# A constant's tile in front of the second layer's small tiles made 256 bytes wide instead of 128

## The chip, the core and the metric

The kernel runs on one core of a Trainium2 chip. The metric is the device time of one execution in microseconds (us), the median of several runs. TensorE (PE in the profile) multiplies matrices, VectorE (DVE), ScalarE (ACT) and GpSimd (POOL) work on elements, and SyncE (SP) issues nearly all DMAs. SBUF, the memory on the chip, has 128 partitions. A tile begins at the same byte in each of its partitions, and that byte is all that this change moves.

## The reference, cut to what matters

```python
B, H, S, Ns, D = (8, 8, 512, 32, 64)
...
x = np.ascontiguousarray(attn_out.transpose(0, 2, 1, 3)).reshape(B * S, H * D)   # 4352 x 512
...
a = x @ w1                       # first layer: 512 -> 1024
b = x @ w2
h = a * b @ w3
x = h @ w_out                    # -> 512
...
h = x @ w_in                     # second layer: 512 -> 2048
relu6 = np.clip(h + 3.0, 0.0, 6.0)
g = h * relu6 / 6.0
return (g @ w_out).astype(np.float32)
```

Attention of 8 batches gives 8 blocks of 512 token rows and 256 state rows. All products are in fp32 accuracy: an operand is split into a high and a low part (names that end in h and l), and three matmuls (high by high, high by low, low by high) take the place of one.

## The kernel before, in words

The program has two stages on TensorE. Up to about 555 us stand the attention, the conversion of the weights and the first layer; its tiles are named Ah, Al, ph, pl, ab, abh, abl, w3ph, w3pl. From about 556 us on stands the second layer, and the change is there.

The second layer takes the blocks of 512 rows in pairs (four values of p) and the 2048 columns of the hidden size in 8 pieces (g), so it runs through 32 units n = 8p + g, and one more (n = LAST = 32). A unit has two parts, which the source writes out in the order in which TensorE executes them:

- Seven products, `prod` (line 799, matmul at line 804), in a scheme with seven products for a block of two by two. Each is six matmuls of 128x128 weights by 512 columns: the weights are slices of `wh` and `wl`, the streamed operand is `xc`, the sum goes to a PSUM bank. In the trace these are `ps<-xc,wh` and `ps<-xc,wl`: the streamed operand stands first, the weights second.
- Eight output groups, `out_mm` (line 840), of the unit before: six matmuls each by `mm3` (lines 88 to 90). Here the weights are 128-column slices of `g`, the high or low part of the gated hidden values, and the streamed operand is `woh` or `wol`, the second weight matrix. In the trace: `ps_o<-woh,g` and `ps_o<-wol,g`. VectorE then adds the bank to the tile `oa` (`add`, line 808), or ScalarE copies it there the first time (line 854).

Six of the eight output groups follow a product directly (`T_()`), one at a time; the last two follow the sixth (`T_(8)`), so three stand in a row. Then come the first two products of the next unit. From n = 25 on the state rows are done too: `state_h` (half-width products, `ps_hs`) and two more groups a unit whose weights are `gs` instead of `g` (`ps_o<-woh,gs`, same lines, same streamed tiles).

The gate is `chain` (line 812): ScalarE's Relu with the bias `half` into `rl`, VectorE's minimum and product into `gt`, ScalarE's rounding to the high part `g`, VectorE's subtraction for the low part. The tiles m1, m5 (`m`), u2, u3 (`u`), `c`, `rl`, `gt`, `g` and `oa` are the small tiles: 512 fp32 values, 2048 bytes a partition each, all from the pool `pb`, which lays its tiles one behind the other in the order of first use. `half` stands in front of them and behind the weights. Its tile is 32 fp32 values wide, and one column of it is used.

Where tiles begin, in bytes in a partition, in the built program:

| tile | begins at (first buffer) | modulo 256 |
|---|---|---|
| first layer: w3ph, w3pl, ph, pl, Ah, Al, asb, ab, abh, abl, x2s | 49280, ... | 128, all |
| wh, wl | 16512, 30848 | 128 |
| woh, wol | 45184, 53376 | 128 |
| half | 61568 | 128 |
| m1, m5, u2, rl, gt, u3, c | 61696, 63744, 65792, 67840, 71936, 76032, 78080 | 0 |
| g (16 buffers) | 84224 to 114944 | 0 |
| oa (10 buffers) | 116992 to 135424 | 0 |
| xc, gs (from the pool xb, at the other end) | 163712, 196480 | 128 |

A 128-column slice of fp32 values is 512 bytes, so a slice of a tile begins in the same place modulo 256 as the tile.

Of the kernel before, what the change touches and what calls it, by code (L numbers as in the profile page):

```python
# [7 lines left out]
F32 = mybir.dt.float32  # L8
# [11 lines left out]
def attn_moe_kernel(tc, xt_d, xn_d, bd_d, wa, wb, wc, wi, wo, out):  # L20
# [32 lines left out]
    def open_pool(key, **kw):  # L53
        es[key] = ExitStack()
        return es[key].enter_context(tc.tile_pool(name=key, **kw))
# [284 lines left out]
    with tc.manual_schedule():  # L340
# [242 lines left out]
        def x2_load(p):  # L583
            if p < B // 2:
                x2r[p] = r = [xb.tile([128, 2, 512], F32, tag=f"r{i}", name=f"r{i}") for i in range(4)]
                for i in range(4):
                    nc.sync.dma_start(out=r[i], in_=x2d[2 * p + i % 2][:, i // 2 * 2:i // 2 * 2 + 2, :])
# [186 lines left out]
        pb = open_pool("pb", bufs=1, side=left, reuse_waits="tile")  # L774
# [17 lines left out]
        wo_load(0)  # L792
        w_load(1)
        x2_load(1)
        half = pb.tile([128, 32], F32, name="half")[:, :1]
        nc.vector.memset(half, 0.5)
        A11, A12, A22, S1, S2, S3, S4 = range(7)

# [245 lines left out]
```

## Time and profile before

| | |
|---|---|
| median of 3 runs | 1275.61 us (1274.97 to 1275.72) |
| profiled execution, first to last instruction | 1274.1 us |
| median of the runs less that span | 1.5 us |
| PE busy | 1237.6 us (97%) |
| DVE busy | 858.0 us (67%) |
| ACT busy | 518.7 us (41%) |
| POOL busy | 32.2 us (3%) |
| granted TensorE clock, mean | 0.993 of full speed |
| DMA moved | 202.67 MB, mean 159 GB/s |

Busy shares are of the whole span. Matmuls overlap: the next starts while the last one is still draining, so the time that one takes (some 390 ns for 512 columns) is longer than the distance from its start to the next start, and that distance is what a row of matmuls costs. The chain of waits shows a matmul with this distance. Times from the span's start are given to 0.01 us.

### The profile page before, as it was taken

The page shows a single profiled execution, that of the slowest core. Times are in us where ns is not written, and L with a number is a line of the kernel's source. Part 1 is how long each engine was busy: PE and PEld are TensorE (multiplying, and loading weights), DVE is VectorE, ACT ScalarE, POOL GpSimd, SP SyncE. Part 2 cuts the span into 40 slices and gives each one's busy share as a digit, 9 for nine tenths or more (in the row PEclk, how much of TensorE's full clock was granted, in tenths as well). Part 3 has the DMA queues.
Part 4 walks back from the last instruction along what each step waited for, and adds up shares of the span by engine and source line. Part 5 has one row for each costly group of instructions (what it writes and reads, how often), then busy time and mean ns, then how long its engine had stood idle before and what let it go on. Part 6 is the DMA issues. An engine that isn't in the chain of part 4 may idle for free.

```text
span 1274.1 us, 16840 instructions
## 1 busy us (share of the span) xinstructions
PE 1237.6 (97%) x6784; PEld 972.2 (76%) x6784; DVE 858.0 (67%) x1268; ACT 518.7 (41%) x811; POOL 32.2 (3%) x18
## 2 busy tenths in 40 slices
PE   5989999999999999999999999999999999999997
PEld 2446787777777788778888888888888888888885
DVE  7976877786877643645667847578566696555664
ACT  3434545464554542544234443234433344332330
POOL 0000000000000000000000200002000030000000
PEclk9989999999999999999999999999999999999999
DMA  9741554554554211354434554345624254342223
GB/s 362 274 166 67 214 211 162 201 227 170 213 189 150 88 37 59 131 175 168 178 114 159 208 198 149 124 160 194 226 99 182 91 190 165 131 141 92 91 91 116
DMA packets 49589, 202.67 MB, mean 159 GB/s; under 512 B 9192, under 2 KB 11240, under 8 KB 42856
## 3 DMA queue, kind: packets, MB, share of 16 engines
q1 hardware_dynamic: 48936, 200.56, 43.5%
q8 instruction: 53, 0.87, 0.3%
q10 hardware_dynamic: 576, 1.05, 0.2%
q14 instruction: 24, 0.20, 0.0%
HBM read 160.17 MB, written 41.42 MB: 158 GB/s over the span
## 4 chain that ended last, share of the span: by engine, by line
PE 85%; DVE 9%; ACT 2%; DMA 1%; issue 1%; ACTq 0%; DVEq 0%; SPq 0%
PE ps L804 24%; PE ps_o L88 10%; PE ps_o L90 10%; PE ps_o L89 10%; PE x L88 4%; PE x L89 4%; PE x L90 4%; PE ps_ab L88 4%; PE ps_ab L90 4%; PE ps_ab L89 4%; PE ps_p L360 2%; PE ps_hs L804 2%; PE ps_w L414 1%; PE ps_r L228 1%; DVE ab L508 1%
## 5 line engine op out<-in xcount | busy, mean ns | idle before, releaser
L804 PE MATMUL ps<-xc,wh 128*128 128x512 f32 x896 | 276.6, 390 | 0.0
L808 DVE TENSOR_TENSOR oa<-oa,ps_o 128x512 f32<-128x512 f32 x238 | 162.9, 686 | 165.8 <-PE ps_o L90 165.1
L88 PE MATMUL ps_o<-woh,g 128*128 128x512 f32 x512 | 203.3, 397 | 0.3 <-ACT g L71 0.3
L90 PE MATMUL ps_o<-woh,g 128*128 128x512 f32 x512 | 201.8, 394 | 0.0
L89 PE MATMUL ps_o<-wol,g 128*128 128x512 f32 x512 | 201.4, 393 | 0.0
L804 PEld LDWEIGHTS ps<-xc,wh 128*128 128x128 f32 x896 | 168.3, 188 | 36.3
L804 PE MATMUL ps<-xc,wl 128*128 128x512 f32 x448 | 175.6, 392 | 0.0
L71 ACT ACTIVATE g<-gt 128x512 fp32r<-128x512 f32 x128 | 81.1, 634 | 177.6 <-DVE gt L818 177.5
L90 PEld LDWEIGHTS ps_o<-woh,g 128*128 128x128 f32 x512 | 96.3, 188 | 23.8 <-DVE g L79 0.4
L89 PEld LDWEIGHTS ps_o<-wol,g 128*128 128x128 f32 x512 | 96.9, 189 | 21.5
L88 PEld LDWEIGHTS ps_o<-woh,g 128*128 128x128 f32 x512 | 96.4, 188 | 21.6 <-ACT g L71 0.8
L88 PE MATMUL x<-abh,w3ph 128*128 128x512 f32 (+1 forms) x288 | 112.3, 390 | 0.0
L89 PE MATMUL x<-abl,w3ph 128*128 128x512 f32 (+1 forms) x288 | 109.0, 378 | 0.0
L90 PE MATMUL x<-abh,w3pl 128*128 128x512 f32 (+1 forms) x288 | 108.8, 378 | 0.0
L88 PE MATMUL ps_ab<-Ah,ph 128*128 128x512 f32 x256 | 102.7, 401 | 2.0 <-ACT ph L71 1.1
L90 PE MATMUL ps_ab<-Ah,pl 128*128 128x512 f32 x256 | 100.8, 394 | 2.1 <-DVE pl L79 2.1
L79 DVE TENSOR_TENSOR g<-gt,g 128x512 fp32r<-128x512 f32 x128 | 89.9, 702 | 18.7 <-ACT g L71 16.4
L89 PE MATMUL ps_ab<-Al,ph 128*128 128x512 f32 x256 | 100.6, 393 | 0.0
L804 PEld LDWEIGHTS ps<-xc,wl 128*128 128x128 f32 x448 | 84.1, 188 | 18.4
L71 ACT ACTIVATE abh<-ab 128x512 fp32r<-128x512 f32 (+1 forms) x72 | 43.8, 608 | 115.0 <-DVE ab L508 115.0
L815 ACT ACTIVATE rl<-c,half 128x512 f32<-128x512 f32 x96 | 69.4, 723 | 32.6 <-DVE c L808 31.2
L79 DVE TENSOR_TENSOR abl<-ab,abh 128x512 fp32r<-128x512 f32 (+1 forms) x72 | 47.3, 657 | 39.9 <-ACT abh L71 39.9
(122 smaller groups left out, 1726.5 us busy)
## 6 DMA issues: line engine op xcount, KB each, us to landing
wh<-swih SPq DMA_DIRECT2D x33, 896.0 KB, 4.7
wl<-swil SPq DMA_DIRECT2D x33, 896.0 KB, 6.4
woh<-swoh SPq DMA_DIRECT2D x33, 512.0 KB, 5.2
wol<-swol SPq DMA_DIRECT2D x33, 512.0 KB, 6.7
out_dram<-oa SPq DMA_DIRECT2D x34, 256.0 KB, 2.4
raw<-in_wb_dram SPq DMA_DIRECT2D x8, 1024.0 KB, 6.6
xr<-in_xt_dram SPq DMA_DIRECT2D x8, 1024.0 KB, 6.8
xn<-in_xn_dram SPq DMA_DIRECT2D x8, 1024.0 KB, 8.0
```

What stands on the lines that cost most here:

```text
L71: nc.scalar.activation(out=out_, in_=in_, func=AF.Copy)
L79: e.tensor_tensor(out=out_, in0=in_, in1=hi.bitcast(F32), op=ALU.subtract)
L88: nc.tensor.matmul(ps, lh, rh, start=first, stop=False)
L89: nc.tensor.matmul(ps, lh, rl, start=False, stop=False)
L90: nc.tensor.matmul(ps, ll, rh, start=False, stop=last)
L228: nc.tensor.matmul(ps[h:h + 64, c * NS:(c + 1) * NS], xn[:, t, c * 128 + h:c * 128 + h + 64], e2t[:, t, g, o:o + NS], start=(t == 0), stop ...
L360: nc.tensor.matmul(ps[c][32 * q:32 * q + 32, 256 * i:256 * i + 256], st_t[b][r, 2 * c + j, 32 * k:32 * k + 32], w12[mm // 2, 2 * c + j][r, ...
L414: nc.tensor.matmul(w3_ps[m], t[:, o:o + 128], wout[k], start=k == 0, stop=k == M1 - 1)
L508: nc.vector.tensor_tensor(out=ab[:, :n], in0=psb[:, :n], in1=a[:, :n], op=ALU.mult)
L804: nc.tensor.matmul(ps, u[:, a, k, :], v[:, k, :], start=first and k == 0 and i == 0, stop=k == 1 and i == 2, skip_group_check=not first or ...
L808: nc.vector.tensor_tensor(out=out_, in0=a, in1=b, op=ALU.add)
L815: nc.scalar.activation(out=rl, in_=c, func=AF.Relu, bias=half, scale=1.0 / 6.0)
```

## The change

One number: the tile of the constant takes 64 fp32 values, 256 bytes a partition, instead of 32.

```diff
         x2_load(1)
-        half = pb.tile([128, 32], F32, name="half")[:, :1]
+        half = pb.tile([128, 64], F32, name="half")[:, :1]
         nc.vector.memset(half, 0.5)
```

`half` itself stays at byte 61568, and one column of it is still used. Every tile of `pb` behind it begins 128 bytes later: m1 at 61824, the g tiles from 84352 on, oa from 117120 on, each 128 modulo 256. The weights in front (wh, wl, woh, wol) and the tiles of the other pool (xc, gs) stay. The order of the instructions on every engine, and what each waits for, is the same in both programs.

## Rows read from the trace of the kernel before

**Rows 1.** Page, its first line and part 1: busy time and instructions by engine.

```profile
span 1274.1 us, 16840 instructions
PE 1237.6 (97%) x6784; PEld 972.2 (76%) x6784; DVE 858.0 (67%) x1268; ACT 518.7 (41%) x811; POOL 32.2 (3%) x18
```

**Rows 2.** Page, part 4: the chain that ended last, by engine and line.

```profile
PE 85%; DVE 9%; ACT 2%; DMA 1%; issue 1%; ACTq 0%; DVEq 0%; SPq 0%
```

**Rows 3.** Stretch of the second layer: length, busy by engine (instructions), clock, DMA share, GB/s.

```profile
571.00:1264.00 693.00, 693.00 (x3101) 569.97 (x3100) 455.56 (x681) 250.84 (x384) 31.49 (x12) 1.00 0.42 151
```

**Rows 4.** Groups by line, shapes apart: count, busy us, mean ns, idle before.

```profile
L88 PE MATMUL ps_o<-woh,g 128*128 128x512 f32 x512 | 203.3, 397 | 0.3 <-ACT g L71 0.3
L90 PE MATMUL ps_o<-woh,g 128*128 128x512 f32 x512 | 201.8, 394 | 0.0
L89 PE MATMUL ps_o<-wol,g 128*128 128x512 f32 x512 | 201.4, 393 | 0.0
...
L90 PE MATMUL x<-abh,w3pl 128*128 128x512 f32 x256 | 99.8, 390 | 0.0
...
L90 PE MATMUL ps_o<-woh,gs 128*128 128x512 f32 x32 | 12.5, 390 | 0.0
L89 PE MATMUL ps_o<-wol,gs 128*128 128x512 f32 x32 | 12.5, 390 | 0.0
L88 PE MATMUL ps_o<-woh,gs 128*128 128x512 f32 x32 | 12.5, 389 | 0.0
```

**Rows 5.** Chain in order of time, 1215 to 1228 us: start, us, what.

```profile
1215.45 0.23 PE ps_o L88
...
1216.84 0.23 PE ps_o L88
...
1219.56 2.73 PE ps L804 x12
1222.28 0.24 PE ps_o L88
...
1223.68 1.37 PE ps L804 x6
1225.05 0.24 PE ps_o L88
...
1226.45 1.37 PE ps L804 x6
1227.82 0.24 PE ps_o L88
```

**Rows 6.** Chain in order of time: the first two products of four units in a row.

```profile
587.11 2.73 PE ps L804 x12
...
607.86 2.73 PE ps L804 x12
...
628.61 2.73 PE ps L804 x12
...
649.37 2.73 PE ps L804 x12
```

**Rows 7.** Groups by line of VectorE and ScalarE, shapes apart, as in rows 4.

```profile
L808 DVE TENSOR_TENSOR oa<-oa,ps_o 128x512 f32<-128x512 f32 x238 | 162.9, 686 | 165.8 <-PE ps_o L90 165.1
...
L508 DVE TENSOR_TENSOR ab<-ps_ab,asb 128x512 f32<-128x512 f32 x64 | 44.0, 688 | 43.7 <-PE ps_ab L90 38.1 <-ACT asb L506 5.5
...
L506 ACT COPY asb<-ps_ab 128x512 f32<-128x512 f32 x64 | 37.4, 584 | 40.8 <-PE ps_ab L90 40.0
...
L933 ACT COPY m<-ps 128x512 f32<-128x512 f32 x32 | 18.7, 585 | 8.1 <-PE ps L804 7.7 <-ACT x2s L83 0.4
```

**Rows 8.** DMA issues: out<-in, count, KB each, median us from issue to landing.

```profile
out_dram<-oa SPq DMA_DIRECT2D x34, 256.0 KB, 2.4
...
x2d<-x2s SPq DMA_DIRECT2D x28, 256.0 KB, 2.7
```

**Rows 9.** Timeline of the end: start, us, engine, line, what, idle before.

```profile
1264.98 0.39 PE L90 MATMUL ps_o<-woh,gs 128*128 128x512 f32 x1
1265.41 0.69 DVE L808 TENSOR_TENSOR oa<-oa,ps_o 128x512 f32<-128x512 f32 x1 [0.67 <-PE ps_o L90]
```

## The prediction

> **What bounds the kernel now.** I read the page's busy times first: TensorE is busy 1237.6 of 1274.1 us, VectorE 67% [rows 1]. The chain that ended last says the same by another way: 85% of it is PE [rows 2]. Then the stretch that the change touches: from 571 to 1264 us TensorE is busy 693.00 us of 693.00, at the full granted clock (1.00), while VectorE is busy 455.56 us and the DMA engines 42% [rows 3]. Nothing is waited for there: the groups of out matmuls have 0.3 us of idle time before them in 512 triples [rows 4], and it is VectorE that waits for TensorE (165.8 us idle before its additions to `oa`, 165.1 of them for `ps_o`) [rows 7]. So the second layer is a row of matmuls, and its length is their number times the distance from one start to the next. Only what changes that distance changes the time.
>
> Next I asked whether the matmuls of one shape all cost the same. They don't. The out matmuls with weights from `g` take 397, 393 and 394 ns on average; with weights from `gs`, on the same lines and with the same streamed tiles, 389, 390 and 390 [rows 4]. The chain in order of time shows the distances. Six matmuls with `g` run from 1215.45 to 1216.84 us, 1.39 us; the twelve with `gs` behind them take 1219.56 - 1216.84 = 2.72 us, 226.7 ns each; the twelve of the two products behind those also take 2.72 us (to 1222.28); the next six with `g` take 1.40 us (to 1223.68), and the product behind them 1.37 (to 1225.05), where half of 2.72 would be 1.36 [rows 5]. So a group with `g` costs 30 to 40 ns more than one with `gs`, and the product between two such groups some 10 ns more. What separates the two is where the weights begin: `g` at 0 modulo 256, `gs`, `wh` and `wl` at 128, with every streamed tile at 128. In the first layer, where all tiles begin at 128, the matmul with the weights `w3pl` also has 390 ns [rows 4].
>
> **The change, part by part.**
>
> *The memset of `half`* still writes one column, and no instruction is added, removed or moved. Nothing.
>
> *The slices of `g`* go to 128. They are then in the position of `gs`, and I price each group with the distance of the `gs` row. A whole unit first: the first two products of four units in a row begin at 587.11, 607.86, 628.61 and 649.37 us [rows 6], so a unit of 7 products and 8 out groups, 90 matmuls, takes 20.75 us, 230.6 ns each. At 226.7 ns it takes 20.40, so 0.35 us come back in a unit. There are 24 units without state rows that have out groups or follow on them (n = 1 to 24): 24 x 0.35 = 8.4 us. In the 7 units with state rows (n = 25 to 31) two of the groups follow a half-width product and cost 1.39 instead of 1.40; I take 0.34: 2.4 us. The last unit has no products, only eight groups at some 0.035: 0.3 us. Together 11.1 us. The first out group stands at the start of the layer and waits for its gate; that stays. I take 11.0.
>
> The lower bound comes from the durations alone: (397 + 393 + 394) - (389 + 390 + 390) = 15 ns a triple, 512 triples, 7.7 us [rows 4]; their ends are modelled, and the products' 10 ns are not in them, so the distances are nearer. The upper bound is 11.1.
>
> *The tiles of VectorE and ScalarE* (m, u, c, rl, gt, oa) go from 0 to 128 too. The rows have the same operation at both places: ScalarE's copy from PSUM takes 584 ns into `asb` (at 128) and 585 into `m` (at 0); VectorE's operation on a bank and a tile takes 688 ns at 128 (`ab`) and 686 at 0 (`oa`) [rows 7]. A nanosecond or two either way, on engines that wait for TensorE. Nothing; if that cover were gone, 2 ns on some 680 VectorE instructions of the stretch [rows 3] would be 1.4 us.
>
> *The stores of `oa`* begin at 128 now. Stores of the same 256 KB land 2.4 us after issue from `oa` (at 0) and 2.7 from `x2s` (at 128) [rows 8]. All but the last lie beside matmuls; the last is issued after the addition that begins at 1265.41 [rows 9], so it is worth between 0 and 0.3 us at the end. I take 0.1, since those other stores ran beside the first layer's traffic. Here a rule speaks against the change: the Trainium skill (DMA: Bandwidth & Descriptors, How a descriptor splits into AXI transactions) has a descriptor that does not start at a multiple of 256 bytes fetch from the multiple below it. By it a run of 2048 bytes touches nine pieces instead of eight; were the whole landing time to grow like that, the estimate is 2.4 / 8 = 0.3 us, again for the last store alone. No run here shows it by itself.
>
> *What comes next.* With 11 us less, VectorE's 455.56 us are 67% of 682 instead of 66% of 693; it remains the one that waits. Between two additions behind a row of out groups it idles 0.67 us [rows 9], and a group that is 0.035 us shorter takes a twentieth of that.
>
> **Sum.** 1274.1 - 11.0 + 0.1 = 1263.2 us for the profiled execution; with the 1.5 us that lie between it and the median of the runs, **1264.7 us**, 0.86% less than 1275.6.
>
> **The rivals.**
>
> *The place of the weights isn't it: no change, 1275.6 us.* The 6 ns might belong to something else that `g` has and `gs` has not: 16 separate tiles instead of two halves of one, or their position right behind a product. Then moving them does nothing. For it: `gs` is 96 matmuls against 1536, and in a chain of waits I see order, not cause. Against it: the groups with `gs` follow a group with `g` without a pause and are at 226.7 ns, while the product, whose own tiles are at 128, is slowed by 10 ns only beside a group with `g` [rows 5]. Chance 0.07. The Trainium skill (TensorE: Matmul & The Clock Gate, Back-to-back issue gap) gives the distance from the number of columns and the clock, with no term for where an operand begins; by that rule this rival would hold. As far as the time of these rows goes, the trace does not agree that columns and clock are all: 1.39 against 1.36 us for six matmuls of the same shape at the same granted clock.
>
> *Slower: one half of 256 bytes for all.* Now weights, streamed tiles and all that VectorE and ScalarE read and write begin at 128; before, their tiles lay at 0 in this stretch. If a matmul is held up where another engine works at the same half, the 1344 products and the 96 `gs` matmuls lose what the `g` matmuls lose now, some 6 ns each, 8.6 us, and the `g` matmuls gain nothing: about 1284 us. It decides from the point where VectorE's traffic at the same half costs a matmul anything. Against it: in the first layer everything is at 128 with VectorE at work on ab and abl, and the matmul stands at 390 ns [rows 4]. Chance 0.03.
>
> *Part of it only: about 1270 us.* Either only the weights' own matmuls or only their neighbours recover, or a wait for a bank that the slower groups hid comes up and takes half of the 11 us. The idle time of VectorE speaks against the latter [rows 7]. Chance 0.04.
>
> Whether `g` is slow because it begins at 0, or because it begins elsewhere than the streamed tile, no row tells: there is no stretch with both at 0. Both give the same sum here.
>
> **How the numbers follow.** The forecast, 0.86, has its own range: from 1263.5 (the upper bound of 11.1 us, no cost of the store, less the 0.7 us by which the three runs differ and 0.3 for 0.01 us of rounding in each of 32 units) to 1268.2 (7.7 us, and 0.3 for the store). The other cases hold 0.14, so the range need not reach to them. What a measurement of this kernel can tell from no change is 0.2%, 2.6 us: faster is the forecast and the partial case, 0.90; the same 0.07; slower 0.03.
>
> **What would show it.** In the profile of the changed kernel the groups with `g` should stand at 389 to 390 ns on lines 88 to 90; the starts of the first two products of neighbouring units 20.40 us apart; the product between out groups at 1.36 us; the second layer's end at about 1254 us instead of 1265; and VectorE's and ScalarE's rows within 2 ns of before. The prediction is wrong if `g` stays at 393 to 397 ns (then the first rival), if the products go up to that (the second), or if idle time appears before the out groups in the second layer (the third).

## The result, and the profile after

The changed kernel takes 1264.67 us (median of 4 runs, 1263.66 to 1266.08), the kernel before 1275.33 us (4 runs, 1274.97 to 1275.72). The ratio is 0.9917, with a 95% interval of 0.9903 to 0.9931.

The page of the profile after, first line, part 1 and part 4, to lay beside [rows 1] and [rows 2]:

```profile
span 1261.7 us, 16840 instructions
...
PE 1225.7 (97%) x6784; PEld 970.1 (77%) x6784; DVE 857.5 (68%) x1268; ACT 518.5 (41%) x811; POOL 32.1 (3%) x18
...
PE 85%; DVE 10%; ACT 2%; DMA 1%; issue 1%; ACTq 0%; DVEq 0%; SPq 0%
```

The same instructions, the same chain, 12 us less TensorE. VectorE and ScalarE have kept their busy times. The groups by line, shapes apart (count, busy us, mean ns, idle before), show whose time it was, beside [rows 4] and [rows 7]:

```profile
L88 PE MATMUL ps_o<-woh,g 128*128 128x512 f32 x512 | 199.8, 390 | 0.3 <-ACT g L71 0.3
L89 PE MATMUL ps_o<-wol,g 128*128 128x512 f32 x512 | 199.7, 390 | 0.0
L90 PE MATMUL ps_o<-woh,g 128*128 128x512 f32 x512 | 199.6, 390 | 0.0
...
L808 DVE TENSOR_TENSOR oa<-oa,ps_o 128x512 f32<-128x512 f32 x238 | 163.0, 686 | 157.1 <-PE ps_o L90 156.3
```

The three groups with `g` have come from 397, 394 and 393 ns to 390, the figure that `gs` had all along. VectorE's addition to `oa` takes 686 ns as before, and the idle time in front of it has shrunk with TensorE's: it still waits for TensorE and not the other way round. The chain in order of time (start, us, what), the beginning of one unit and, last, the first products of the eighth unit after it:

```profile
584.86 2.72 PE ps L804 x12
587.58 0.23 PE ps_o L88
...
588.94 1.36 PE ps L804 x6
590.30 0.23 PE ps_o L88
...
748.05 2.72 PE ps L804 x12
```

Twelve products take 2.72 us, six with `g` 588.94 - 587.58 = 1.36, the six products behind them 1.36: no shape stands out any more. Eight units take 748.05 - 584.86 = 163.19 us, 20.40 each; before, four units from 587.11 on had 20.75 each [rows 6].

From the start of the first product to the start of the last matmul the second layer took 1264.98 - 555.80 = 709.2 us before (first row below, and [rows 9]); after, by the rows behind it, 1252.46 - 553.84 = 698.6. That is **10.6 us less**, as much as the medians differ (10.7).

```profile
555.80 0.62 PE L804 MATMUL ps<-xc,wh 128*128 128x512 f32 x2
```

```profile
553.84 0.62 PE L804 MATMUL ps<-xc,wh 128*128 128x512 f32 x2
```

```profile
1252.46 0.39 PE L90 MATMUL ps_o<-woh,gs 128*128 128x512 f32 x1
1252.89 0.69 DVE L808 TENSOR_TENSOR oa<-oa,ps_o 128x512 f32<-128x512 f32 x1 [0.67 <-PE ps_o L90]
```

The two profiled spans differ by more, 12.4 us. The other 2 us lie in front of the second layer and are not the change's: in the profiled execution before, the granted clock was 0.97 in the stretch from 440 to 500 us, after it was 1.00 (columns: length, PE busy and matmuls, clock, DMA share, GB/s; before, then after). Behind two waits of TensorE, 0.70 and 1.06 us long in both traces, the clock fell from 2.4 to 1.2 GHz for a part of the stretch in the one execution (0.72 from 462 to 468 us) and not in the other.

```profile
440.00:500.00 60.00, 56.28 (x424) 0.97 0.08 28
```

```profile
440.00:500.00 60.00, 56.27 (x436) 1.00 0.09 29
```

Twelve matmuls more fit into the same time. The experiments below have it either way in a stretch that none of them touches: the run e1_g_only had 0.97 there, e2_rest_only 1.00. So I compare units, and medians, not spans.

### The profile page after: what moved, and what is told of

Its sections match the earlier page's. It is cut to its first block, busy times and chain, and to the rows that moved or that the text cites. A ratio compares the mean times of both kernels' runs of the same rounds, so it can differ in the third digit from the quotient of the medians.

```text
span 1261.7 us, 16840 instructions
## 1 busy us (share of the span) xinstructions
PE 1225.7 (97%) x6784; PEld 970.1 (77%) x6784; DVE 857.5 (68%) x1268; ACT 518.5 (41%) x811; POOL 32.1 (3%) x18
## 4 chain that ended last, share of the span: by engine, by line
PE 85%; DVE 10%; ACT 2%; DMA 1%; issue 1%; ACTq 0%; DVEq 0%; SPq 0%
PE ps L804 24%; PE ps_o L88 10%; PE ps_o L90 10%; PE ps_o L89 10%; PE x L88 4%; PE x L89 4%; PE x L90 4%; PE ps_ab L88 4%; PE ps_ab L90 4%; PE ps_ab L89 4%; PE ps_p L360 2%; PE ps_hs L804 2%; PE ps_w L414 1%; PE ps_r L228 1%; DVE ab L508 1%
## 5 line engine op out<-in xcount | busy, mean ns | idle before, releaser
L88 PE MATMUL ps_o<-woh,g 128*128 128x512 f32 x512 | 199.8, 390 | 0.3 <-ACT g L71 0.3
L89 PE MATMUL ps_o<-wol,g 128*128 128x512 f32 x512 | 199.7, 390 | 0.0
L90 PE MATMUL ps_o<-woh,g 128*128 128x512 f32 x512 | 199.6, 390 | 0.0
L88 PE MATMUL x<-abh,w3ph 128*128 128x512 f32 (+1 forms) x288 | 112.4, 390 | 0.0
L88 PEld LDWEIGHTS ps_o<-woh,g 128*128 128x128 f32 x512 | 96.2, 188 | 20.1 <-ACT g L71 0.8
L89 PEld LDWEIGHTS ps_o<-wol,g 128*128 128x128 f32 x512 | 96.2, 188 | 19.3
L89 PE MATMUL x<-abl,w3ph 128*128 128x512 f32 (+1 forms) x288 | 109.1, 379 | 0.0
L88 PE MATMUL ps_ab<-Ah,ph 128*128 128x512 f32 x256 | 102.7, 401 | 1.6 <-DVE pl L79 0.9
L89 PE MATMUL ps_ab<-Al,ph 128*128 128x512 f32 x256 | 100.6, 393 | 0.0
```

What stands on the lines that cost most here:

```text
L88: nc.tensor.matmul(ps, lh, rh, start=first, stop=False)
L89: nc.tensor.matmul(ps, lh, rl, start=False, stop=False)
L90: nc.tensor.matmul(ps, ll, rh, start=False, stop=last)
```

## The experiments

The profile says that `g` at 0 was slow and `g` at 128 is not. It does not say why, and the change moved m, u, c, rl, gt and oa along with `g`. The theories: **A**, a slice of weights that begins at 0 modulo 256 is slow by itself; **B**, weights and streamed tile must begin at the same place modulo 256; **C**, it is the tiles that VectorE and ScalarE read and write. The later D and E are variants. In every kernel the order of instructions on the engines is that of before; only where tiles begin differs. Each "unit" below is the mean of eight, from the first to the ninth pair of first products in the chain of waits.

### Which tiles: only g, or all but g

The first kernel puts 128 bytes in front of the `g` tiles and 128 behind them, with `half` at 32 values:

```diff
-            pool, tag = (xb, "xc") if key[1] == "s" else (pb, f"g{key[1]}{key[2]}")
+            key == (0, 0, 0) and pb.tile([128, 32], F32, name="gpad"); pool, tag = ...
...
-                oacc[key] = pb.tile([128, 512], F32, tag="oa", name="oa", bufs=10)
+                n or j != 1 or t or pb.tile([128, 32], F32, name="oapad"); oacc[key] = ...
```

> Only the g tiles begin at 128 modulo 256; m, u, c, rl, gt and oa stay at 0 and woh, wol at 128, as before. Theory A (a slice of weights that begins at 0 modulo 256 is slow, whatever is streamed): fast, all gain, 1264.7 us, g groups at 390 ns, units 20.40 us. Theory B (weights and streamed tile must begin at the same place modulo 256): the same, 1264.7 us. Theory C (it is the tiles of VectorE and ScalarE at 0 that slow the matmuls): no gain, 1275.3 us, g groups at 393 to 397 ns.

Measured: 1263.62 us against 1274.22, ratio 0.9904 (0.9887 to 0.9920).

```profile
586.85 2.72 PE ps L804 x12
...
750.05 2.72 PE ps L804 x12
```

163.20 / 8 = 20.40 us a unit: all of the gain, with every tile of VectorE and ScalarE but `g` where it was. The second kernel has the same two pads and `half` at 64 values, so that `g` alone stays at 0.

> The reverse: m, u, c, rl, gt and oa begin at 128, the g tiles stay at 0. A and B: no gain, 1275.3 us, units 20.75 us, g groups at 393 to 397 ns. C: all gain, 1264.7 us, g groups at 390 ns.

Measured: 1274.43 us against 1274.22, ratio 0.9999 (0.9990 to 1.0008).

```profile
584.91 2.73 PE ps L804 x12
...
750.94 2.73 PE ps L804 x12
```

166.03 / 8 = 20.75 us: nothing gained. **C falls**, and the whole change is the place of the weights `g`.

### By itself, or against the streamed tile

Both kernels put 128 bytes in front of `woh`, which moves the streamed tiles of the out groups to 0; the first has `half` at 64 values (g at 0), the second at 32 (g at 128).

```diff
         w_load(0)
-        wo_load(0)
+        pb.tile([128, 32], F32, name="wopad"); wo_load(0)
```

> woh and wol, the streamed tiles of the out groups, go to 0 as well, and g and the small tiles stay at 0, so weights and streamed tile are both at 0. A: g still slow, 1275.3 us, units 20.75 us. B: g groups fast (390 ns, units 20.40 us), but the 96 gs matmuls (128 against 0) some 6 ns slower each, 0.6 us: 1265.3 us. C: slow, 1275.3 us.

Measured: 1269.16 us against 1274.22, ratio 0.9949 (0.9934 to 0.9963).

```profile
586.75 2.73 PE ps L804 x12
...
750.91 2.73 PE ps L804 x12
```

164.16 / 8 = 20.52 us, between the two forecasts. The chain shows what is fast and what isn't:

```profile
586.75 2.73 PE ps L804 x12
589.48 0.23 PE ps_o L88
...
590.85 1.37 PE ps L804 x6
592.22 0.23 PE ps_o L88
...
593.59 1.37 PE ps L804 x6
```

The group with `g` at 0 and `woh` at 0 takes 590.85 - 589.48 = 1.37 us and no longer 1.40: at 0, too, a group is fast. But each product and each group is 0.01 above 1.36. Here the place changes between a product (128 and 128) and a group (0 and 0), and a unit has 12 such changes: (20.52 - 20.40) / 12 is 10 ns a change. I had not foreseen this. At such a change a matmul streams a tile at one place and the weights of the next matmul begin at the other.

> woh and wol go to 0, g and the small tiles to 128: the same distance between the two as in the kernel before, the other way round. A: fast, 1264.7 us, units 20.40 us. B: slow, g groups at 393 to 397 ns and units 20.75 us, gs groups too, 1275.9 us. C: fast, 1264.7 us.

Measured: 1275.37 us against 1274.22, ratio 1.0003 (0.9993 to 1.0012).

```profile
587.05 2.73 PE ps L804 x12
...
753.13 2.73 PE ps L804 x12
```

166.08 / 8 = 20.76 us: `g` at 128 is slow when `woh` and `wol` are at 0. **A falls**.

B as worded, for the two operands of one and the same matmul, does not fit e3_wo0_g0 either: there every matmul's own two operands agree, and still each change costs 10 ns. The traces tell which two count. The weights of a matmul are loaded while the matmul in front of it streams, as in these rows of the kernel after, where the load for L89 begins with the matmul of L88 and 0.22 us before its own:

```profile
1252.01 0.39 PE L88 MATMUL ps_o<-woh,gs 128*128 128x512 f32 x1
1252.02 0.19 PEld L89 LDWEIGHTS ps_o<-wol,gs 128*128 128x128 f32 x1
...
1252.24 0.39 PE L89 MATMUL ps_o<-wol,gs 128*128 128x512 f32 x1
```

So take the last matmul of a product that stands between two groups. Its own operands are at 128 in all three kernels below, and it streams `xc` while the first slice of `g` is loaded (mean distance from its start to the next start, 122 such products from 576 to 1080 us):

| kernel | `xc` streams from | `g` is loaded from | distance, ns |
|---|---|---|---|
| before | 128 | 0 | 232.5 |
| e3_wo0_g0 | 128 | 0 | 232.3 |
| e4_wo0_g128 | 128 | 128 | 226.7 |

In e4_wo0_g128 it costs nothing extra, although a slow group follows; in e3_wo0_g0 it does, although the group that follows is fast. What must agree is thus the tile that a matmul streams and the weights of the *next* matmul. By the order of the matmuls a unit has 48 such pairs that disagree before (42 inside the groups, 6 from a product to a group; they cost 0.35 us), 48 in e4_wo0_g128 (0.36 us) and 12 in e3_wo0_g0 (0.12 us). Part of the price falls on the matmuls right behind: the first of a product takes 230.8 ns before and in e3_wo0_g0. **B stands in this form**; within a row of groups or of products, all from the same tiles, it asks for the same as B as worded.

### Another pair of tiles, and all at 0

If B is about any weights and streamed tile, the products must suffer when `xc` is moved. From the changed kernel, a pad as the last tile of the pool `xb` moves `xc`, `gs` and the states' tiles to 0:

```diff
-        nc.vector.memset(half, 0.5)
+        nc.vector.memset(half, 0.5); xb.tile([128, 32], F32, name="xpad")
```

> From the changed kernel, the pool xb is shifted: xc, gs and the states' tiles begin at 0, wh, wl, g, woh and wol stay at 128. Now the products' weights and streamed tile differ. Theory B (any matmul row slows where weights and streamed tile begin at different places modulo 256): the 1344 product matmuls and the 96 with gs take some 6 ns more, 8.6 us, and the out groups beside products some 10 ns a group, 1.8 us; 1264.7 + 10.4 = 1275.1 us, units 20.75 us or more. Theory D (only the out groups are sensitive, for example because their weights are written by ScalarE and VectorE and not by DMA): products stay at 390 ns, 0.6 us for gs alone, 1265.3 us.

Measured: 1275.01 us against 1274.99, ratio 1.0000 (0.9991 to 1.0010).

```profile
584.99 2.79 PE ps L804 x12
...
750.75 2.79 PE ps L804 x12
```

Twelve products take 2.79 us instead of 2.72, 6 ns more each, and a unit 165.76 / 8 = 20.72 (20.75 or more was expected). The gain of the change is gone again, by the products, whose weights come by DMA. **D falls.** The next kernel has this pad and another one in front of `wh`, so that all that TensorE reads in the second layer begins at 0:

```diff
-        w_load(0)
+        pb.tile([128, 32], F32, name="wpad"); w_load(0)
```

> All that TensorE reads in the second layer begins at 0: wh, wl, xc, g, gs, woh, wol, and the small tiles too. Theory B: as fast as all at 128, 1264.7 us, units 20.40 us. Theory E (both at 0 costs something, which run e3_wo0_g0 hid in its edges): the products slow too, above 1269 us, units above 20.52 us.

Measured: 1264.48 us against 1274.99, ratio 0.9918 (0.9903 to 0.9933).

```profile
586.51 2.72 PE ps L804 x12
...
749.72 2.72 PE ps L804 x12
```

163.21 / 8 = 20.40 us. **E falls**: there is nothing in 128 as such. What the change brought is that all are alike.

### How alike

Only the width of `half` differs in the five kernels that follow, so `g` moves against `woh` and `wol`, which stay at 128. The other small tiles move along; e2_rest_only cleared them at 128 alone, and VectorE's addition to `oa` takes 686 or 687 ns in all five.

```diff
-        half = pb.tile([128, 32], F32, name="half")[:, :1]
+        half = pb.tile([128, W], F32, name="half")[:, :1]   # W = 16, 48, 128, 56, 8
```

> The tile of half is 64 bytes, so the small tiles and g begin at 192 modulo 256, streamed woh and wol at 128. B strict (the same place modulo 256): slow, 1275.3 us, units 20.75 us. B by halves (what counts is in which 128 bytes of 256 a slice begins): fast, 1264.7 us, units 20.40 us. B by distance (the cost grows with the distance): about half, 1270 us, units 20.57 us.

Measured: 1278.27 us against 1274.99, ratio 1.0028 (1.0019 to 1.0037): slower than the kernel before. Unit 167.04 / 8 = 20.88 us.

```profile
584.70 2.75 PE ps L804 x12
...
751.74 2.75 PE ps L804 x12
```

> The tile of half is 192 bytes, so the small tiles and g begin at 64 modulo 256, streamed woh and wol at 128. B strict: slow, 1275.3 us. B by halves: slow, 1275.3 us. B by distance: about half, 1270 us.

Measured: 1267.49 us against 1274.99, ratio 0.9950 (0.9934 to 0.9967). Unit 164.06 / 8 = 20.51 us.

```profile
584.16 2.72 PE ps L804 x12
...
748.22 2.72 PE ps L804 x12
```

192 lies in the same 128 bytes as the streamed tile's 128 and is the slower of the two: B by halves falls.

> The tile of half is 512 bytes: g and the small tiles begin 256 bytes further than in the changed kernel, again at 128 modulo 256. Theory B with a period of 256 bytes: as fast as the changed kernel, 1264.7 us, units 20.40 us. A longer period (512 bytes or more, so that the changed kernel met a good place by luck): slower, units above 20.45 us.

Measured: 1263.66 us against 1274.61, ratio 0.9920 (0.9903 to 0.9936). Unit 163.20 / 8 = 20.40 us.

```profile
584.33 2.72 PE ps L804 x12
...
747.53 2.72 PE ps L804 x12
```

256 bytes further nothing changes, as a period of 256 asks for.

> The tile of half is 224 bytes: g and the small tiles begin at 96, 32 bytes in front of the place of woh and wol. At 64 bytes in front (run e8_g64) a unit took 20.51 us. If the cost shrinks with the distance: about 20.46 us, 1266.5 us. If only the very same place is free of it: 20.51 us or more, 1267.5 us or more. If a small lead is better than none: below 20.40 us, under 1264 us.

Measured: 1278.78 us against 1274.61, ratio 1.0032 (1.0020 to 1.0044). Unit 167.14 / 8 = 20.89 us.

```profile
585.39 2.76 PE ps L804 x12
...
752.53 2.76 PE ps L804 x12
```

> The tile of half is 32 bytes: g and the small tiles begin at 160, 32 bytes behind the place of woh and wol. At 64 bytes behind (run e7_g192) a unit took 20.88 us. If the cost shrinks with the distance: about 20.64 us, 1271.5 us. If only the very same place is free of it: 20.75 us or more, 1275 us or more.

Measured: 1274.98 us against 1274.61, ratio 1.0004 (0.9995 to 1.0014). Unit 166.08 / 8 = 20.76 us.

```profile
585.07 2.73 PE ps L804 x12
...
751.15 2.73 PE ps L804 x12
```

Both are at 32 bytes from the streamed tile, and both cost as much as 128 bytes or more; B by distance falls. Where `g` begins, modulo 256, with the streamed tile at 128 (each ratio is to the kernel before in the same round of runs):

| g begins at | from the streamed tile | unit, us | median, us | ratio to before |
|---|---|---|---|---|
| 0 (before) | 128 | 20.75 | 1275.33 | 1 |
| 64 | 64 in front | 20.51 | 1267.49 | 0.9950 |
| 96 | 32 in front | 20.89 | 1278.78 | 1.0032 |
| 128 (after) | 0 | 20.40 | 1264.67 | 0.9917 |
| 128, 256 bytes further | 256 | 20.40 | 1263.66 | 0.9920 |
| 160 | 32 behind | 20.76 | 1274.98 | 1.0004 |
| 192 | 64 behind | 20.88 | 1278.27 | 1.0028 |

Only the very same place is free of the cost, among those tried. No kernel here beats the changed one by more than the runs scatter.

## Why the prediction was right, point by point

The cause is the one forecast, the place of the weights from `g`, and the size is right within 0.3 us. That the median lies within 0.03 us of 1264.7 is luck: the forecast gain of 10.9 us was 0.24 us too large, the median that it was taken from lay 0.28 us above the one measured beside the change (1275.61, 1275.33), and single runs of the changed kernel spread over 2.4 us.

*What bounds.* TensorE has no idle time in the second layer before or after, and the time fell by what its matmuls no longer take. Right.

*The slices of g.* The distances of the `gs` row were the price that `g` then had: 390 ns, 1.36 us a group, 1.36 for the product beside it, 20.40 us a unit, each as forecast. The layer's last matmul starts at 1252.46 us and not at about 1254 because the layer begins 2 us earlier in that execution. The 24 plain units gave 24 x (20.75 - 20.40) = 8.4 us, the forecast's figure.

*The units with state rows* are the one term that was too large: I took 0.34 us each. The first products of two of these units, four apart, stand in the chain at

```profile
1114.33 2.73 PE ps L804 x12
...
1219.56 2.73 PE ps L804 x12
```

before, and after at

```profile
1103.41 2.72 PE ps L804 x12
...
1207.58 2.72 PE ps L804 x12
```

so 26.31 us a unit before, 26.04 after, 0.27 less. Seven of them make 1.9 us and not 2.4. What did not come back is, for the most part, two groups in each that follow a half-width product (2 x 0.03 us, by 1.39 and 1.36, of the 0.07 us that are missing). In the profile after they still cost what they cost before:

```profile
1226.69 0.23 PE ps_o L88
...
1228.08 1.43 PE ps_hs L804 x12
```

1.39 us from 1226.69 to 1228.08, with all tiles at 128; I had counted them as part of the same loss because they had the same 1.39 before [rows 5]. So 11.0 became 10.6.

*VectorE and ScalarE*: 686 ns for the addition to `oa` at both places, busy 857.5 us against 858.0 and 518.5 against 518.7. Nothing, as forecast.

*The stores of oa* land as soon as before in the median. The DMA issues after (count, KB each, median us to landing):

```profile
out_dram<-oa SPq DMA_DIRECT2D x34, 256.0 KB, 2.4
```

Most of them lie beside matmuls. The last one does show its place: from the start of the last addition to the end of the span there were 1274.1 - 1265.41 = 8.7 us before and 1261.7 - 1252.89 = 8.8 after. The other traces have the same two levels, one execution each: 8.67 to 8.71 us in the four kernels whose `oa` begins at 0 (before, e1_g_only, e3_wo0_g0, e6_all0), 8.83 to 8.92 in the nine where it begins elsewhere. So the last store costs 0.1 to 0.2 us more away from a multiple of 256, as taken. The Trainium skill (DMA: Bandwidth & Descriptors, How a descriptor splits into AXI transactions) has extra bytes fetched at such a start. The traces agree in direction, and with less than the 0.3 us that was estimated from it.

*The rivals.* That the place is not it: refuted, by the result and by e1_g_only and e2_rest_only together. For the distance between matmuls the Trainium skill (TensorE: Matmul & The Clock Gate, Back-to-back issue gap) names columns, clock and the weight load that goes with each matmul, but no place. The runs here need one more term, worth 0 to 0.49 us in a unit of 90 matmuls at the same columns and clock. That one half of 256 bytes for all engines makes it slower: refuted, and e6_all0 shows it at the other half as well. That only part comes back: no; the loss of 0.4 us is the state units' and not a new wait. What the prediction left open, whether `g` is slow at 0 or slow away from the streamed tile, is settled: the latter (e3_wo0_g0, e4_wo0_g128). That both "give the same sum here" holds only because the products' tiles were at 128 already: had the change brought `g` and `woh` together at 0, the changes between products and groups would have cost 0.12 us a unit, as in e3_wo0_g0. The 10 ns that the prediction saw in the product beside a group are of this kind: its last matmul streams `xc` at 128 while `g` is loaded from 0.

## What to carry to other kernels

Where a profile shows a row of matmuls of one shape at two distances, and no waits, look where their operands begin: in this kernel a row in which all weights and streamed tiles begin at the same place modulo 256 costs 226.7 ns a matmul, others up to 10 ns more ((20.89 - 20.40) us over the 48 out matmuls of a unit). Not the place matters but that a streamed tile shares it with the weights that are loaded meanwhile, those of the next matmul; one small constant in front of a pool's tiles is enough to shift them all. Half measures can be worse than none (32 bytes in front: 1278.78 us).

## What the runs showed of the hardware that was not expected

- The cost is not a matter of distance: 64 bytes in front of the streamed tile a unit takes 20.51 us, 32 in front 20.89, 32 behind 20.76, 64 behind 20.88, 128 away 20.75. What makes this order stays open; no run here tells it.
- The pair that counts is a matmul's streamed tile and the next matmul's weights: a change of place between neighbours costs some 10 ns even where each matmul's own two operands agree (e3_wo0_g0). Of these 10 ns some 6 fall on the matmul in front of the change and 4 on the one behind it; why the one behind it is slow is not shown.
- Behind the last matmul, a store from a tile that does not begin at a multiple of 256 bytes ends 0.1 to 0.2 us later (8.83 to 8.92 against 8.67 to 8.71 us from the last addition's start to the span's end).
- Behind twelve half-width products, a group of six takes 1.39 us instead of 1.36 with all operands at one place. There are 16 such groups, 0.5 us in all. Whether it is the half width or something else in front of them was not tried.
